# Attention scores on 64-row tiles of TensorE, q and k transposed in one block, and the sink columns of P taken off GpSimd, in a fused attention and two-MoE kernel

## The chip, the core and the metric

The kernel runs as one program on one core of a Trainium2 chip. The metric is the device time of one execution in microseconds (us), the median of several runs. TensorE is called PE here (its weight loads PEld), VectorE DVE, ScalarE ACT, GpSimd POOL, and SyncE, whose queue issues most DMAs, SP.

## What is computed

```python
def reference(...):                         # B=4, H=8, S=768, D=64; sinks 4, window 128
    scores = q @ k.T / sqrt(D)              # per batch and head
    keep   = (key < 4) | (0 <= query - key < 128)
    a = softmax(where(keep, scores, -1e9))
    x = (a @ v)  as 3072 tokens x 512
    x = ((x @ w1) * (x @ w2)) @ w3 @ w_out  # w1, w2: 512x1024; w3: 1024x1024; w_out: 1024x512 (float64 in DRAM)
    logits = x @ w_gate + bias[modality];  e = argmax;  gate = softmax(logits)[e]      # 8 experts
    out = gate * (relu(x @ W1[e]) @ W2[e])  # W1: 512x1024, W2: 1024x512, float32
```

## The kernel before, in words

Products are kept near float32 by splitting each operand into a rounded high part and a rest ("low"), both in the type fp32r, and adding three products: high*high, high*low, low*high. ACT makes the high part, DVE the low one.

The program has four stages, which the profile shows one after the other. **Start** (0 to 129 us): the float64 weights are loaded (`f64_load`), turned into float32 on DVE (`f64_to_f32`), and w3 times w_out is formed on PE (`product`, L289). **First MoE** (129 to 708 us): six groups of 512 tokens; per group 192 matmuls of x with w1 and w2 (L703, tile ab) and 96 with the product of the weights (L691, tile x2p). **Experts** (708 us to the end): seven slots, six of 512 tokens and one of 128; a slot reads which expert and which tokens it has (`decide`, tk and tab), gathers its rows (L859), transposes them (L899), and multiplies by W1 (L912) and W2 (L949), whose parts are loaded as wst by SP (L868, L870). Between them **routing** steps (`route`) compute logits on DVE (L764) and ranks on PE (tile rk).

Attention is cut in 48 units n: 12 stretches of 256 queries by 4 pairs of heads. `att_stream` yields five steps a unit, and the driver `front` weaves them into the start and the first five groups, so that units 0 to 7 fall mostly into the start. A unit before the change: split q and k (`a_split`), transpose the parts with four fp32r transposes each (`a_tq`, `a_tk`), copy q a second time with its halves exchanged (`a_swap`), add the four sink keys to k (kT, on POOL), form scores for two blocks j of 128 queries (`a_scores`: four matmuls each, in which high and low lie on the two halves of the 128 rows), softmax to P, gather P's sink columns as three parts on POOL (psk, L485 and L488) and transpose them (L492), transpose the rest of P (`a_pt`), and multiply by v (`a_pv`: L531, whose two heads write the two halves of the PSUM partitions, and L534 for the sinks).

Within an engine instructions run in the order that the scheduler wrote; a waiting instruction holds all behind it.

Of the kernel before, what the change touches and what calls it, by code (L numbers as in the profile page):

```python
# [26 lines left out]
def attention_moe_moe_kernel(ctx, tc, q, k, v, w1, w2, w3, w_out, mod_id, w_gate, mod_bias, e_w1, e_w2, out,  # L27
# [16 lines left out]
    NS = 4  # L44
    KW = 128 + NS
    banded = n_sink == NS and window == 128

# [46 lines left out]
    neg_r = const.tile([128, 128], F32R, name="neg_r")  # L94
    cur_i = const.tile([128, 128], I32, name="cur_i")
# [12 lines left out]
    ksk = const.tile([128, H, NS], F32R, name="ksk")  # L108
    psk = const.tile([128, 2, 96], F32R, name="psk")
    vst = const.tile([96, NP, 128], F32, name="vst")  # L110

    def consts_early():
# [5 lines left out]
        nc.vector.tensor_scalar(out=neg_r, in0=idf, scalar1=-1.0, scalar2=None, op0=ALU.mult)  # L118
        nc.gpsimd.memset(tmp, 1.0)
# [10 lines left out]
        nc.gpsimd.memset(psk.bitcast(F32), 0.0)  # L130
# [206 lines left out]
    carry = {}  # L337
    xb = mm.tile([128, NP, 2, 3, UNIT], F32R, tag="xb", bufs=1, name="xb")

    def a_load(n):  # L340
        u, p = divmod(n, NP)
        b, c = divmod(u, NC)
        hs = slice(2 * p, 2 * p + 2)
        qn = att.tile([128, 2, 2, D], F32, tag="qn", bufs=2, name="qn")
        kn = att.tile([128, 2, 2, D], F32, tag="kn", bufs=2, name="kn")
        for src, dst in ((q, qn), (k, kn)):
            for j in range(2):
                s0 = c * UNIT + j * 128
                nc.sync.dma_start(out=dst[:, :, j], in_=src[b, hs, s0:s0 + 128, :].rearrange("h s d -> s h d"))
        nat[n] = (qn, kn)  # L350

    def a_load_v(n):
        u, p = divmod(n, NP)
        b, c = divmod(u, NC)
        hs = slice(2 * p, 2 * p + 2)
        vn = att.tile([128, 3, 2, D], F32, tag="vn", bufs=2, name="vn")
# [4 lines left out]
        if c == 0 and p == 0:  # L361
            for kind in range(3):
                for h in range(2):
                    r = kind * 32 + h * NS
                    nc.sync.dma_start(out=vst[r:r + NS, :, h * D:(h + 1) * D],
                                      in_=v[b].rearrange("(p h) s d -> h s p d", h=2)[h, 0:NS])
# [7 lines left out]
    def a_split(n):  # L374
        qn, kn = nat.pop(n)
        qs = att.tile([128, 4, 2, D], F32R, tag="qs", bufs=1, name="qs")
        ks = att.tile([128, 4, 2, D], F32R, tag="ks", bufs=1, name="ks")
        qf = qn.rearrange("p h j d -> p (h j) d")
        kf = kn.rearrange("p h j d -> p (h j) d")
        nc.scalar.activation(out=qs[:, :, 0, :], in_=qf, func=ACTF.Copy, scale=1.0 / float(D) ** 0.5)  # L380
        nc.scalar.activation(out=ks[:, :, 0, :], in_=kf, func=ACTF.Copy)

        def low_parts():
            nc.vector.scalar_tensor_tensor(out=qs[:, :, 1, :], in0=qf, scalar=1.0 / float(D) ** 0.5,
                                           in1=f32(qs[:, :, 0, :]), op0=ALU.mult, op1=ALU.subtract)
            nc.vector.tensor_tensor(out=ks[:, :, 1, :], in0=kf, in1=f32(ks[:, :, 0, :]), op=ALU.subtract)

        stt["low", n] = defer(low_parts)
        stt["s", n] = (qs, ks)

    def a_tq(n):
        qs, ks = stt["s", n]
        stt.pop(("low", n))()
# [3 lines left out]
        qT = att.tile([128, 4, 128], F32R, tag="qT0", bufs=2, name="qT")  # L397
        nc.scalar.activation(out=qT, in_=f32(tp), func=ACTF.Copy)
        stt["q", n, 0] = qT
        stt["tq", n] = tp  # L400

    def a_swap(n):
        qW = att.tile([128, 4, 128], F32R, tag="qT1", bufs=2, name="qW")
        tp = stt.pop(("tq", n))
        for x in range(2):
            nc.scalar.activation(out=qW[x * D:(x + 1) * D], in_=f32(tp[(1 - x) * D:(2 - x) * D]), func=ACTF.Copy)
        stt["q", n, 1] = qW

    def a_tk(n):
        u, p = divmod(n, NP)  # L410
        b, c = divmod(u, NC)
        qs, ks = stt.pop(("s", n))
        tp = ps_t.tile([128, 4, 128], F32R, tag="t", name="tk")
        for i in range(4):
            nc.tensor.transpose(out=tp[:, i, :], in_=ks[:, i].rearrange("p a d -> p (a d)"), identity=idr)
        kT = att.tile([128, 2, 3, KW], F32R, tag="kT", bufs=1, name="kT")
        for h in range(2):
            nc.scalar.activation(out=kT[:, h, 1:3, NS:KW], in_=f32(tp[:, 2 * h:2 * h + 2, :]), func=ACTF.Copy)
        if c == 0:
            nc.gpsimd.tensor_copy(out=ksk[:, 2 * p:2 * p + 2, :], in_=f32(kT[:, :, 1, NS:2 * NS]))  # L420
        s0 = 0 if c else 1
        nc.gpsimd.tensor_copy(out=kT[:, :, s0:3, 0:NS],
                              in_=f32(ksk[:, 2 * p:2 * p + 2, :]).unsqueeze(2).to_broadcast([128, 2, 3 - s0, NS]))
        if c:
            nc.vector.tensor_copy(out=kT[:, :, 0, NS:KW], in_=f32(carry[p]))
        if c < NC - 1:
            cr = att.tile([128, 2, 128], F32R, tag=f"carry{p}", bufs=1, name="carry")
            nc.vector.tensor_copy(out=cr, in_=f32(kT[:, :, 2, NS:KW]))
            carry[p] = cr
        stt["k", n] = kT  # L430

    def a_scores(n, j):
        u, p = divmod(n, NP)
        b, c = divmod(u, NC)
        kT = stt["k", n]
        sp = ps_s.tile([128, 2, 512], F32, tag="s", name="sp")
        blk0 = c == 0 and j == 0
        s0 = 1 if blk0 else j
        for h in range(2):
# [12 lines left out]
        else:  # L452
            nc.vector.copy_predicated(out=sp[:, :, NS:KW], mask=cur_i.unsqueeze(1).to_broadcast([128, 2, 128]),
# [10 lines left out]
        def norm():  # L464
            r = st[:, 2]
            nc.vector.tensor_scalar(out=st[:, 1], in0=st[:, 1], scalar1=1.0e-9, scalar2=None, op0=ALU.add)
            nc.vector.reciprocal(out=r, in_=st[:, 1])
            nc.vector.tensor_tensor(out=P[:, j, :, lo:KW], in0=P[:, j, :, lo:KW],  # L468
# [4 lines left out]
    def a_sk(n):  # L473
# [5 lines left out]
        j0 = 0 if c else 1  # L479
        xp = ps_x.tile([128, 2, 256], F32, tag="x", name="xp")  # L480
        stt["x", n] = xp
        pk = psk.rearrange("p j (a r) -> p j a r", a=3)
        nj = 2 - j0
        for kind in (0, 2):
            nc.gpsimd.tensor_copy(out=pk[:, j0:2, kind, 0:2 * NS].rearrange("p j (h k) -> p j h k", h=2),  # L485
                                  in_=P[:, j0:2, :, 0:NS])
        for j in range(j0, 2):
            nc.gpsimd.tensor_tensor(out=pk[:, j, 1, 0:2 * NS].rearrange("p (h k) -> p h k", h=2),  # L488
                                    in0=P[:, j, :, 0:NS],
                                    in1=f32(pk[:, j, 0, 0:2 * NS]).rearrange("p (h k) -> p h k", h=2),  # L490
                                    op=ALU.subtract)
            nc.tensor.transpose(out=xp[0:96, 1, j * 128:(j + 1) * 128].bitcast(F32R), in_=psk[:, j, :], identity=idr)  # L492
        pt = att.tile([96, 256], F32R, tag="pskT", bufs=1, name="pskT")
        nc.scalar.activation(out=pt[:, j0 * 128:256], in_=xp[0:96, 1, j0 * 128:256], func=ACTF.Copy)
# [23 lines left out]
    def a_pv(n):  # L518
# [5 lines left out]
        sk = stt.pop(("sk", n))  # L524
        spans = [(1, slice(0, 256), parts.rearrange("p a j h q -> p (a j) h q")[:, 0:4:3]),
# [3 lines left out]
        for x, (vj, cols, pm) in enumerate(spans):  # L529
            for h in range(2):  # L530
# [4 lines left out]
                         start=False, stop=True, skip_group_check=True)  # L535
        xh, xl = xb[:, p, 0, u % 3], xb[:, p, 1, u % 3]
        nc.scalar.activation(out=xh, in_=xp[:, 0], func=ACTF.Copy)  # L537
        defer(lambda: nc.vector.tensor_tensor(out=xl, in0=xp[:, 0], in1=f32(xh), op=ALU.subtract))
        stt.pop(("k", n)); stt.pop(("q", n, 0)); stt.pop(("q", n, 1))
# [6 lines left out]
    def att_stream():  # L546
        a_load(0)
        a_load_v(0)
        a_load(1)
        a_vsink(0)  # L550
        a_split(0)
        a_tq(0)
        a_swap(0); yield
        a_tk(0); yield
        for n in range(NN):
            if n + 2 < NN:
                a_load(n + 2)
            if n + 1 < NN:
                a_split(n + 1)
# [4 lines left out]
            if n + 1 < NN:  # L564
                a_tq(n + 1)
                a_swap(n + 1)
# [7 lines left out]
            if n + 1 < NN:  # L574
                a_tk(n + 1); yield
        a_sk(NN - 1); a_pt(NN - 1); yield
        a_pv(NN - 1)
# [415 lines left out]
    def front():  # L993
# [17 lines left out]
        t = 0.0  # L1011
        f64_ahead(4)
# [202 lines left out]
```

## Time and profile before

| what | value |
|---|---|
| median of 3 runs (range) | 1012.94 us (1012.55 to 1014.28) |
| the profiled execution: its time, its span | 1017.59 us, 1015.9 us |
| busy in the span: PE, PEld | 956.0 us (94%), 752.5 us (74%) |
| busy in the span: DVE, ACT, POOL | 644.0 us (63%), 515.8 us (51%), 218.0 us (21%) |
| granted TensorE clock, mean share of full | 0.987 |

The span runs from the first to the last instruction. The end of a matmul is modelled and a matmul overlaps the next, so what a matmul costs PE is read from start to start.

### The profile page before, as it was taken

How to read it: one execution, taken by the hardware profiler on the slowest of the kernel's cores; microseconds unless marked ns; L12 is line 12 of the kernel's file. 1: busy time of each engine (PE TensorE's matmuls, PEld its weight loads, DVE VectorE, ACT ScalarE, POOL GpSimd, SP SyncE). 2: the span in 40 equal slices, each digit the busy share in tenths (PEclk: the TensorE clock that was granted, in tenths of full speed). 3: DMA queues.
4: the chain of work that ended last, by engine and by line, in shares of the span. 5: the costliest groups of instructions: out<-in, count | busy, mean ns of one | idle time of the engine just before them, and what ended most of it. 6: DMA issues, size and time to landing. Idle time of an engine off the chain costs nothing. (4 is left out here: it accounts for less than half of the span.)

```text
span 1015.9 us, 16038 instructions
## 1 busy us (share of the span) xinstructions
PE 956.0 (94%) x4976; PEld 752.5 (74%) x4976; DVE 644.0 (63%) x1968; ACT 515.8 (51%) x1354; POOL 218.0 (21%) x460
## 2 busy tenths in 40 slices
PE   4899799999999999999999999999999997999995
PEld 2667578867786778678867886778888886888884
DVE  7788796489638963895489639847934354343432
ACT  3689665576447644774576445314433414343433
POOL 1232312113223221222122222222031222021010
PEclk9899999999999999999999999999999998999998
DMA  8665624112202220222022200452445306343331
GB/s 262 188 171 167 188 69 131 23 45 63 58 19 49 58 55 19 56 61 52 16 50 59 58 9 16 129 80 63 145 166 117 133 13 236 125 146 117 122 116 52
DMA packets 125417, 94.05 MB, mean 93 GB/s; under 512 B 96712, under 2 KB 105160, under 8 KB 125201
## 3 DMA queue, kind: packets, MB, share of 16 engines
q1 hardware_dynamic: 120560, 80.12, 28.3%
q0 software_dynamic: 4768, 12.88, 4.2%
q8 instruction: 40, 0.66, 0.3%
q14 instruction: 49, 0.39, 0.2%
HBM read 80.14 MB, written 13.09 MB: 92 GB/s over the span
## 5 line engine op out<-in xcount | busy, mean ns | idle before, releaser
L703 PE MATMUL ab<-xb,wab 128*128 128x512 f32 x1152 | 291.0, 397 | 0.4 <-DVE g L713 0.3
L703 PEld LDWEIGHTS ab<-xb,wab 128*128 128x128 f32 x1152 | 210.6, 189 | 41.9 <-ACT xb L537 1.2
L949 PE MATMUL x<-w 128*128 128x512 f32 x600 | 143.1, 396 | 0.0
L764 DVE CUSTOM_DVE_ANT_0 junk<-rows,wgb 128x512 bf16<-128x512 f32 x192 | 134.8, 702 | 1.5 <-ACT rows L751 0.6
L949 PEld LDWEIGHTS x<-w 128*128 128x128 f32 x600 | 113.1, 190 | 23.7 <-DVE w L196 0.3
L691 PE MATMUL x2p<-w3o,gh 128*128 128x512 f32 x384 | 128.2, 407 | 0.0
L461 ACT ACTIVATE P<-sp,st 128x132 f32<-128x132 f32 (+1 forms) x192 | 69.2, 368 | 40.4 <-DVE st L459 26.4
L196 DVE TENSOR_TENSOR w<-wst,w 128x512 fp32r<-128x512 f32 x112 | 71.5, 683 | 25.1 <-ACT w L195 25.1
L513 POOL TENSOR_SCALAR_AFFINE_SELECT ptp<-ptf 128x512 f32<-128x512 f32 (+1 forms) x96 | 63.7, 688 | 107.8 <-ACT ptf L508 107.8
L691 PE MATMUL x2p<-w3o,gl 128*128 128x512 f32 x192 | 76.4, 400 | 0.0
L691 PEld LDWEIGHTS x2p<-w3o,gh 128*128 128x128 f32 x384 | 66.9, 188 | 11.8 <-ACT gh L680 1.9
L912 PE MATMUL ab<-w,w 128*128 128x512 f32 x288 | 75.1, 396 | 0.0
L916 DVE SCALAR_TENSOR_TENSOR w<-ab,w 128x512 fp32r<-128x512 f32 x48 | 33.1, 690 | 65.6 <-ACT w L915 65.4
L195 ACT ACTIVATE w<-wst 128x512 fp32r<-128x512 f32 x112 | 63.5, 628 | 20.9 <-DMA wst<-in_moe_w_dram 20.9
L912 PE MATMUL ab<-w 128*128 128x512 f32 x288 | 74.0, 392 | 0.0
L953 POOL DMA_INDIRECT out_dram<-late,ti x25 | 25.6, 1026 | 217.1 <-ACT late L952 193.0
L680 ACT ACTIVATE gh<-g 128x256 fp32r<-128x256 f32 x96 | 39.9, 415 | 63.0 <-DVE g L710 48.1
L710 DVE TENSOR_TENSOR g<-ab,bs 128x256 f32<-128x256 f32 x48 | 20.2, 421 | 76.6 <-PE ab L703 76.5
L485 POOL CAST psk<-P 128x16 fp32r<-128x16 f32 (+1 forms) x96 | 23.7, 276 | 202.1 <-DVE P L468 149.6
L915 ACT ACTIVATE w<-ab 128x512 fp32r<-128x512 f32 x48 | 28.8, 599 | 74.5 <-PE ab L912 74.1
L912 PEld LDWEIGHTS ab<-w,w 128*128 128x128 f32 x288 | 54.0, 188 | 13.0
L912 PEld LDWEIGHTS ab<-w 128*128 128x128 f32 x288 | 54.0, 188 | 12.1
(195 smaller groups left out, 1685.7 us busy)
## 6 DMA issues: line engine op xcount, KB each, us to landing
wst<-in_moe_w_dram SPq DMA_DIRECT2D x56, 512.0 KB
f64st<-in_moe_w_dram SPq DMA_DIRECT2D x32, 512.0 KB
vn<-in_v_dram SPq DMA_DIRECT2D x128, 64.0 KB
xs<-rows SPq DMA_DIRECT2D x12, 513.0 KB
qn<-in_q_dram SPq DMA_DIRECT2D x96, 64.0 KB
kn<-in_k_dram SPq DMA_DIRECT2D x96, 64.0 KB
f64st<-in_moe_w_out_dram SPq DMA_DIRECT2D x8, 512.0 KB
wgb<-wgt SPq DMA_DIRECT2D x1, 2048.0 KB
```

Of the source, the lines that this page charges most:

```text
L195: nc.scalar.activation(out=hi, in_=src, func=ACTF.Copy)
L196: lo_eng.tensor_tensor(out=lo, in0=src, in1=f32(hi), op=ALU.subtract)
L461: nc.scalar.activation(out=P[:, j, h, lo:KW], in_=sp[:, h, lo:KW], func=ACTF.Exp, bias=st[:, 0, h:h + 1], accum_out=st[:, 1, h:h + 1])
L513: nc.gpsimd.affine_select(out=parts[:, a, i0:2].rearrange("p j h q -> p (j h) q"), in_=full[:, 2 * i0:4], pattern=[[0, 4 - 2 * i0], [sign, ...
L680: nc.scalar.activation(out=gh, in_=g, func=ACTF.Copy)
L691: nc.tensor.matmul(out=x2p[t], lhsT=a[:, sl], rhs=b_, start=(f == 0 and i == 0), stop=(f == KF - 1 and i == 2))
L703: nc.tensor.matmul(out=bank[nm].rearrange("p (u t) -> p u t", u=2), lhsT=a, rhs=b_, start=(kk == 0 and i == 0), stop=(kk == KD - 1 and i = ...
L764: nc.vector.tensor_tensor_reduce(out=junk, in0=rows[:, t, 0:DM], in1=wgb[0][:, e, :], scale=1.0, scalar=0.0, op0=ALU.mult, op1=ALU.add, ac ...
L912: nc.tensor.matmul(out=hp, lhsT=a[:, fs], rhs=b_, start=(kk == 0 and i == 0), stop=(kk == KD - 1 and i == 2))
L915: nc.scalar.activation(out=h[:, 0], in_=hp, func=ACTF.Relu)
L916: nc.vector.scalar_tensor_tensor(out=h[:, 1], in0=hp, scalar=0.0, in1=f32(h[:, 0]), op0=ALU.max, op1=ALU.subtract)
L949: nc.tensor.matmul(out=op, lhsT=a[:, ts], rhs=b_, start=(f == 0 and i == 0), stop=(f == KF - 1 and i == 2))
```

## The change

Five edits, in one diff of some 250 lines.

1. q and k are transposed as loaded, in float32, four transposes into one PSUM bank (`a_tqk`), and split afterwards, out of PSUM. The tiles of k live on in a ring of three blocks per head pair, so nothing is carried over by DVE; the sink keys are copied by POOL once for each batch and pair.
2. The scores take three matmuls per head and block in place of two, each with 64 rows: head 0 on partitions 0 to 63, head 1 on 64 to 127. The first block of a batch has 132 columns instead of 264.
3. P's sink columns are gathered by ACT into a tile skn of 8 columns, transposed in float32 to 8 partitions, and split out of PSUM by two ACT copies and one DVE subtraction (`a_skT`, a step of its own place).
4. For units 0 to 7 (`n < FEW`) the low parts of q, k and x come from PE and ACT (a matmul with a negative identity into the same bank, then a copy), and P is normalised on ACT.
5. The loads of unit 0 go out before the second pair of float64 weights; in the last group routing steps and the decisions of slots 1 to 3 come later, and those of slots 4 to 6 move from slot 2 into slot 3.

```diff
-    def a_tq(n):
-        tp = ps_t.tile([128, 4, 128], F32R, tag="t", name="tq")
-        for i in range(4):
-            nc.tensor.transpose(out=tp[:, i, :], in_=qs[:, i].rearrange("p a d -> p (a d)"), identity=idr)
...
+    def a_tqk(n):
+        tp = ps_t.tile([128, 4, 128], F32, tag="t", name="tqk")
+        for x, src in enumerate((qn, kn)):
+            for j in range(2):
+                i = j if x == 0 or s0 < s1 else 1 - j
+                nc.tensor.matmul(out=tp[:, 2 * x + i], lhsT=src[:, j], rhs=idf, is_transpose=True, start=(x + j == 0),
+                                 stop=(x + j == 2), skip_group_check=True)
...
+            if n < FEW:
+                nc.tensor.matmul(out=tp[:, 0:2], lhsT=negq_r, rhs=qh, start=False, stop=True, skip_group_check=True)
...
-        for h in range(2):
-            for part in range(2):
-                nc.tensor.matmul(out=sp[:, h, 0:2 * KW], lhsT=stt["q", n, part][:, 2 * h + j, :],
-                                 rhs=kT[:, h, s0:s0 + 2, :].rearrange("p a b -> p (a b)"),
-                                 start=(part == 0), stop=(part == 1))
+        for i, (a, b_) in enumerate(((qh, 0), (ql, 0), (qh, 1))):
+            for h in range(2):
+                hp = slice(h * D, (h + 1) * D)
+                nc.tensor.matmul(out=sp[:, h, 0:nk].rearrange("p (a b) -> p a b", b=KW), lhsT=a[hp, j, :],
+                                 rhs=kr[hp, b_, blocks, :], start=(i == 0), stop=(i == 2))
...
-            nc.tensor.transpose(out=xp[0:96, 1, j * 128:(j + 1) * 128].bitcast(F32R), in_=psk[:, j, :], identity=idr)
...
+    def a_skT(n):
...
+            nc.tensor.transpose(out=xp[0:2 * NS, 1, j * 128:(j + 1) * 128], in_=skn[:, j], identity=idf)
...
-            if pos == N_EARLY - 2:
...
+                    if pos == N_EARLY - 1 and f == 2:
```

The order on PE, a unit in the first group of the first MoE (ab and x2p are the MoE's own matmuls; the last figures are output partitions by columns). Before:

```order
L703 MATMUL ab<-xb,wab 128x512 x9
L396 MATMUL tq<-idr,qs 128x128 x4
L691 MATMUL x2p<-w3o,gh 128x512 x2
L691 MATMUL x2p<-w3o,gl 128x512
L441 MATMUL sp<-kT,qT 128x264
L441 MATMUL sp<-kT,qW 128x264
L703 MATMUL ab<-xb,wab 128x512 x12
L531 MATMUL xp<-ptp,vn 64x256 x2
L531 MATMUL xp<-ptp,vn 64x128 x4
L534 MATMUL xp<-pskT,vsk 128x256
L415 MATMUL tk<-idr,ks 128x128 x4
```

And with the change, at the same place:

```order
L715 MATMUL ab<-xb,wab 128x512 x7
L396 MATMUL tqk<-idf,qn 128x128 x2
L396 MATMUL tqk<-idf,kn 128x128 x2
L499 MATMUL xp<-idf,skn 8x128 x2
L703 MATMUL x2p<-w3o,gh 128x512 x2
L443 MATMUL sp<-ring,qh 128x264 x2
L443 MATMUL sp<-ring,ql 128x264 x2
L715 MATMUL ab<-xb,wab 128x512 x12
L543 MATMUL xp<-ptp,vn 64x256 x2
L543 MATMUL xp<-ptp,vn 64x128 x4
L546 MATMUL xp<-pskT_108,vsk 128x256
```

The transposes of k (tk) are gone, the sink transposes stand beside those of q and k, and a block of scores has six matmuls of half the rows (three rows of two) in place of four.

SP's order at the end of slot 2 (wst are expert weights, `TENSOR_LOAD dri` reads a decision and waits for it, tk the token lists). Before:

```order
L870 DMA wst<-in_moe_w_dram 128x2x512
L839 TENSOR_LOAD dri
L840 TENSOR_LOAD dri
L846 DMA tk<-tab_70 128x4
L846 DMA tk<-tab_71 128x4
L1168 TENSOR_LOAD tri
L868 DMA wst<-in_moe_w_dram 128x1024
```

And with the change:

```order
L880 DMA wst<-in_moe_w_dram 128x1024
L882 DMA wst<-in_moe_w_dram 128x2x512
L851 TENSOR_LOAD dri
L852 TENSOR_LOAD dri
L1183 TENSOR_LOAD tri
L858 DMA tk<-tab_70 128x4
L858 DMA tk<-tab_71 128x4
```

The W1 loads of slot 3 (L868 before, L880 now) stood behind the decisions and lists of slots 4 to 6 and now stand ahead of them; rows that repeat are shown once.

## Rows read from the trace of the kernel before

**Rows 1.** Busy time by stage: start (two parts) and first MoE.
```profile
core 0: us, PE busy (x) PEld busy (x) DVE busy (x) ACT busy (x) POOL busy (x), PEclk, DMA share, GB/s
0.00:50.00 50.00, 31.96 (x130) 22.38 (x131) 38.86 (x84) 24.99 (x58) 8.12 (x25) 0.93 0.71 223
50.00:129.00 79.00, 71.18 (x434) 54.08 (x432) 64.31 (x170) 61.38 (x172) 23.57 (x49) 0.98 0.60 172
129.00:633.00 504.00, 492.14 (x2786) 382.17 (x2784) 353.84 (x1204) 294.11 (x874) 116.79 (x294) 1.00 0.20 49
```
**Rows 2.** Groups on PE: busy us, mean ns | idle before, with releasers.
```profile
L441 PE MATMUL sp<-kT,qT 128*128 128x264 f32 x192 | 54.9, 306 | 4.1 <-POOL kT L422 3.6 <-issue 0.3
L531 PE MATMUL xp<-ptp,vn 128*64 128x256 f32 x192 | 36.4, 405 | 3.6 <-POOL ptp L513 3.5
L492 PE MATMUL xp<-idr,psk 128*96 128x128 f32 x80 | 16.1, 249 | 14.7 <-POOL psk L488 14.5
```
**Rows 3.** Timeline of PE in the first MoE: start, length, what, count.
```profile
402.65 0.45 PE L396 MATMUL tq<-idr,qs 128*128 128x128 f32 x4
402.94 0.69 PE L691 MATMUL x2p<-w3o,gh 128*128 128x512 f32 x2
403.47 0.40 PE L691 MATMUL x2p<-w3o,gl 128*128 128x512 f32 x1
...
404.40 0.29 PE L441 MATMUL sp<-kT,qT 128*128 128x264 f32 x1
...
404.89 0.63 PE L691 MATMUL x2p<-w3o,gh 128*128 128x512 f32 x2
...
406.05 0.40 PE L691 MATMUL x2p<-w3o,gl 128*128 128x512 f32 x1
406.37 0.65 PE L531 MATMUL xp<-ptp,vn 128*64 128x256 f32 x2
406.95 0.74 PE L691 MATMUL x2p<-w3o,gh 128*128 128x512 f32 x2
407.53 0.40 PE L691 MATMUL x2p<-w3o,gl 128*128 128x512 f32 x1
```
**Rows 4.** Timeline of PE: a whole product with v, in the start.
```profile
110.65 1.09 PE L531 MATMUL xp<-ptp,vn 128*64 128x256 f32 x12
111.67 0.39 PE L534 MATMUL xp<-pskT,vsk 96*128 96x256 f32 x1
111.89 0.46 PE L415 MATMUL tk<-idr,ks 128*128 128x128 f32 x4
```
**Rows 5.** Timeline of PE: float32 transposes of an expert slot.
```profile
741.84 0.60 PE L899 MATMUL x<-idf,late 128*128 128x128 f32 x4
742.27 0.60 PE L899 MATMUL t<-idf,late 128*128 128x128 f32 x4
```
**Rows 6.** Timeline of PE: the old sink transposes.
```profile
411.78 0.28 PE L492 MATMUL xp<-idr,psk 128*96 128x128 f32 x2
411.89 0.62 PE L504 MATMUL pt<-idf,P 128*128 128x128 f32 x4
```
**Rows 7.** Waits after 640 us: engine line <- releaser: total us, times, longest.
```profile
PE x L899 <- DVE w L196: 5.6, 1, 5.6
PE rk L786 <- DVE oh L775: 2.6, 1, 2.6
```
**Rows 8.** Three stretches with a low granted clock (columns as in rows 1).
```profile
121.50:125.00 3.50, 3.50 (x12) 2.68 (x12) 0.00 (x0) 0.86 (x2) 1.22 (x2) 0.51 0.87 296
660.80:664.20 3.40, 3.06 (x12) 2.48 (x12) 3.05 (x23) 0.60 (x1) 2.77 (x3) 0.51 0.68 30
845.00:851.00 6.00, 4.79 (x16) 4.12 (x17) 5.53 (x9) 4.57 (x9) 2.62 (x3) 0.51 0.91 312
```
**Rows 9.** Timeline of SP's queue at the end of slot 2.
```profile
827.47 8.60 SPq L846 DMA_DIRECT2D tk<-tab  x6
836.94 7.36 SPq L868 DMA_DIRECT2D wst<-in_moe_w_dram  x4
```
**Rows 10.** Groups on DVE in the start, 0 to 129 us.
```profile
L468 DVE TENSOR_TENSOR P<-P,st 128x264 f32<-128x264 f32 x13 | 5.6, 427 | 0.2
L384 DVE SCALAR_TENSOR_TENSOR qs<-qn,qs 128x256 fp32r<-128x256 f32 x10 | 5.1, 514 | 0.0
```

More of the change, by code (lines that the diff above doesn't have):

```diff
@@ L107, in attention_moe_moe_kernel @@
     eidx, ebase, done, tot = (dec[:, x] for x in range(4))
-    ksk = const.tile([128, H, NS], F32R, name="ksk")
-    psk = const.tile([128, 2, 96], F32R, name="psk")
+    pskT = [const.tile([96, 256], F32R, name=f"pskT{x}") for x in range(2)]
     vst = const.tile([96, NP, 128], F32, name="vst")
@@ L129, in consts_early @@
         nc.vector.tensor_copy(out=past_i, in_=tmp)
-        nc.gpsimd.memset(psk.bitcast(F32), 0.0)
+        for x in pskT:
+            nc.gpsimd.memset(x.bitcast(F32), 0.0)
         nc.gpsimd.memset(vst, 0.0)
@@ L360, in a_load_v, with a_load_sinks @@
         stt["v", n] = vn
-        if c == 0 and p == 0:
-            for kind in range(3):
-                for h in range(2):
-                    r = kind * 32 + h * NS
-                    nc.sync.dma_start(out=vst[r:r + NS, :, h * D:(h + 1) * D],
-                                      in_=v[b].rearrange("(p h) s d -> h s p d", h=2)[h, 0:NS])
+        if n and c == 0 and p == 0:
+            a_load_sinks(b)
+    def a_load_sinks(b):
+        for kind in range(3):
+            for h in range(2):
+                r = kind * 32 + h * NS
+                nc.sync.dma_start(out=vst[r:r + NS, :, h * D:(h + 1) * D],
+                                  in_=v[b].rearrange("(p h) s d -> h s p d", h=2)[h, 0:NS])
     def a_vsink(b):
@@ L372, in a_vsink @@
         stt["vsk", b] = vsk
[L374 to L389, printed above, removed]
@@ L409, in a_tk, with low_parts, sinks @@
-    def a_tk(n):
+    def a_tqk(n):
         u, p = divmod(n, NP)
         b, c = divmod(u, NC)
[L412 to L430, printed above, removed]
+        qn, kn = nat.pop(n)
+        if n < NP:
+            ring.append(att.tile([128, 2, 3, KW], F32R, tag=f"ring{p}", bufs=1, name="ring"))
+        kr = ring[p]
+        s0, s1 = 2 * c % 3, (2 * c + 1) % 3
+        blocks = slice(s0, s1 + 1) if s0 < s1 else slice(s1, s0 + 1, s0 - s1)
+        tp = ps_t.tile([128, 4, 128], F32, tag="t", name="tqk")
[4 more added lines that the diff above has]
+                                 stop=(x + j == 2), skip_group_check=True)
+        qh = att.tile([128, 2, 128], F32R, tag="qh", bufs=2, name="qh")
+        ql = att.tile([128, 2, 128], F32R, tag="ql", bufs=2, name="ql")
+        scale = 1.0 / float(D) ** 0.5
+        nc.scalar.activation(out=qh, in_=tp[:, 0:2], func=ACTF.Copy, scale=scale)
+        nc.scalar.activation(out=kr[:, 0, blocks, NS:KW], in_=tp[:, 2:4], func=ACTF.Copy)
+        def low_parts():
+            if n < FEW:
+                nc.tensor.matmul(out=tp[:, 0:2], lhsT=negq_r, rhs=qh, start=False, stop=True, skip_group_check=True)
+                nc.tensor.matmul(out=tp[:, 2:4], lhsT=neg_r, rhs=kr[:, 0, blocks, NS:KW], start=False, stop=True,
+                                 skip_group_check=True)
+                nc.scalar.activation(out=ql, in_=tp[:, 0:2], func=ACTF.Copy, scale=scale)
+                nc.scalar.activation(out=kr[:, 1, blocks, NS:KW], in_=tp[:, 2:4], func=ACTF.Copy)
+                sinks()
+                return
+            nc.vector.scalar_tensor_tensor(out=ql, in0=tp[:, 0:2], scalar=scale, in1=f32(qh), op0=ALU.mult,
+                                           op1=ALU.subtract)
+            nc.vector.tensor_tensor(out=kr[:, 1, blocks, NS:KW], in0=tp[:, 2:4], in1=f32(kr[:, 0, blocks, NS:KW]),
+                                    op=ALU.subtract)
+            sinks()
+        def sinks():
+            if c == 0:
+                nc.gpsimd.tensor_copy(out=kr[:, :, :, 0:NS],
+                                      in_=f32(kr[:, :, 0, NS:2 * NS]).unsqueeze(2).to_broadcast([128, 2, 3, NS]))
+        stt["low", n] = defer(low_parts)
+        stt["q", n] = (qh, ql)
@@ L434, in a_scores @@
         b, c = divmod(u, NC)
-        kT = stt["k", n]
+        if j == 0:
+            stt.pop(("low", n))()
+        kr = ring[p]
+        qh, ql = stt["q", n]
         sp = ps_s.tile([128, 2, 512], F32, tag="s", name="sp")
+        cur = (2 * c + j) % 3
         blk0 = c == 0 and j == 0
-        s0 = 1 if blk0 else j
-        for h in range(2):
-            for part in range(2):
-                nc.tensor.matmul(out=sp[:, h, 0:2 * KW], lhsT=stt["q", n, part][:, 2 * h + j, :],
-                                 rhs=kT[:, h, s0:s0 + 2, :].rearrange("p a b -> p (a b)"),
-                                 start=(part == 0), stop=(part == 1))
+        wrapped = cur == 0 and not blk0
+        blocks = slice(0, 1) if blk0 else slice(0, 3, 2) if wrapped else slice(cur - 1, cur + 1)
+        nk = KW if blk0 else 2 * KW
+        for i, (a, b_) in enumerate(((qh, 0), (ql, 0), (qh, 1))):
+            for h in range(2):
+                hp = slice(h * D, (h + 1) * D)
+                nc.tensor.matmul(out=sp[:, h, 0:nk].rearrange("p (a b) -> p a b", b=KW), lhsT=a[hp, j, :],
+                                 rhs=kr[hp, b_, blocks, :], start=(i == 0), stop=(i == 2))
         if j == 0:
@@ L452, in a_scores @@
         else:
-            nc.vector.copy_predicated(out=sp[:, :, NS:KW], mask=cur_i.unsqueeze(1).to_broadcast([128, 2, 128]),
+            other = past_i if wrapped else cur_i
+            nc.vector.copy_predicated(out=sp[:, :, NS:KW], mask=other.unsqueeze(1).to_broadcast([128, 2, 128]),
                                       data=sp[:, :, KW + NS:2 * KW])
@@ L467, in norm @@
             nc.vector.reciprocal(out=r, in_=st[:, 1])
+            if n < FEW:
+                for h in range(2):
+                    nc.scalar.activation(out=P[:, j, h, lo:KW], in_=P[:, j, h, lo:KW], func=ACTF.Copy,
+                                         scale=r[:, h:h + 1])
+                return
             nc.vector.tensor_tensor(out=P[:, j, :, lo:KW], in0=P[:, j, :, lo:KW],
@@ L479, in a_sk @@
         j0 = 0 if c else 1
+        skn = att.tile([128, 2, 2 * NS], F32, tag="skn", bufs=2, name="skn")
+        nc.scalar.activation(out=skn[:, j0:2].rearrange("p j (h k) -> p j h k", h=2), in_=P[:, j0:2, :, 0:NS],
+                             func=ACTF.Copy)
+        stt["skn", n] = skn
+    def a_skT(n):
+        c = n // NP % NC
+        skn = stt.pop(("skn", n))
         xp = ps_x.tile([128, 2, 256], F32, tag="x", name="xp")
         stt["x", n] = xp
[L482 to L494 removed]
+        cols = slice(0 if c else 128, 256)
+        for j in range(0 if c else 1, 2):
+            nc.tensor.transpose(out=xp[0:2 * NS, 1, j * 128:(j + 1) * 128], in_=skn[:, j], identity=idf)
+        pt = pskT[n % 2]
+        src = xp[0:2 * NS, 1, cols]
+        for kind in (0, 2):
+            nc.scalar.activation(out=pt[kind * 32:kind * 32 + 2 * NS, cols], in_=src, func=ACTF.Copy)
+        stt["sklo", n] = defer(lambda: nc.vector.tensor_tensor(out=pt[32:32 + 2 * NS, cols], in0=src, in1=f32(pt[0:2 * NS, cols]),
+                                                               op=ALU.subtract))
         stt["sk", n] = pt
@@ L1128, in back @@
                     route_step()
-            if pos == N_EARLY - 2:
-                while route_step():
-                    pass
-                for x in range(N_LATE + 1):
-                    slots.append(Slot(SLOT if x < N_LATE else 128, NT, mem))
-                    slots[-1].decide()
-                cnt = trips(p2a_pool[0])
-                n = len(slots)
-                order += list(range(N_EARLY, n))
+                    if pos == N_EARLY - 1 and f == 2:
+                        while route_step():
+                            pass
+                        for x in range(N_LATE + 1):
+                            slots.append(Slot(SLOT if x < N_LATE else 128, NT, mem))
+                            slots[-1].decide()
+                        cnt = trips(p2a_pool[0])
+                        order += list(range(N_EARLY, len(slots)))
             nx = slots[order[pos + 1]] if pos + 1 < len(order) else None
```

67 lines of the change are left out of this document (33 added, 34 removed).

## The prediction

> **What bounds the kernel now.** First read the busy time by stage, to see which engine a stage leans on. In the first MoE PE is busy 492.14 of 504 us, DVE 353.84, ACT 294.11, POOL 116.79 [rows 1]: PE sets that stage, and work taken off the others counts only where PE waits for it. In the start it is mixed: up to 50 us PE is busy 31.96 us against DVE's 38.86, from 50 to 129 us PE 71.18 of 79, DVE 64.31, ACT 61.38 [rows 1].
>
> Then the groups of PE, whose last column is the idle time just before them. POOL's hand in the sink columns costs 14.5 us in front of the sink transposes, 3.6 in front of the scores (sink keys) and 3.5 in front of the product with v [rows 2]. The waits of the last third show two more: 2.6 us for the ranks of a routing step and 5.6 us before the transposes of slot 3 [rows 7]. After these holes the granted clock drops to its lower level, 1.2 GHz: three stretches of 3.4 to 6 us stand at 0.51 [rows 8]. In the first of them PE had just idled for the sink columns, in the second for the ranks, in the third for slot 3.
>
> Last the timeline of PE, since a busy share says nothing of what a matmul costs. Starts, not lengths, are to be compared.
> - Matmuls of 512 columns: from 404.89 to 406.05 there are five (two, and three in rows left out), 1.16 us, 0.23 each [rows 3].
> - Four score matmuls: 404.40 to 404.89, 0.49 us, with nothing lost before or after [rows 3].
> - Four fp32r transposes: 402.65 to 402.94, 0.29, and the next two matmuls take 0.53 instead of twice 0.23: 0.36 together [rows 3].
> - Four float32 transposes: 741.84 to 742.27, 0.43, so 0.11 each [rows 5].
> - Two old sink transposes: 411.78 to 411.89, 0.11 [rows 6].
> - The product with v is the one that shows what tiles of less than 128x128 cost. Two matmuls of 64 output columns stand alone at 406.37. The matmul before started at 406.05 and would have left PE at 406.28; the two after them started at 406.95 and the next at 407.53, 0.58 instead of 0.46, so the stream was whole again as if from 407.07. That is 0.79 us. The two themselves need 0.44 (256 columns at twice the 0.11 us of 128 float32 columns). The rest, 0.35, goes for the change into the narrow tile and back, some 0.18 a change [rows 3, 5].
> - A whole product of 12 such matmuls (4 of 256 and 8 of 128 columns) takes 110.65 to 111.67, 1.02 us, where one after the other would be 1.76 and two heads at a time 0.88 [rows 4]. So two tiles on different halves do run together.
>
> **The change part by part, in PE's time.**
>
> *q and k.* One block of four float32 transposes (0.43) for two blocks of fp32r ones (0.72): -0.29 in 48 units, -14 us.
>
> *Scores, the stream alone.* A block goes from four matmuls (0.49) to six with half the rows. No row of before has tiles of 64 rows. Bounds: the halves run together, three times 0.12 = 0.36; or one after the other, 0.72. I take the first, by the nearest row, the two heads of the product with v [rows 4]. 80 blocks by -0.13 are -10 us; the 16 blocks of 132 columns lie between 0.18 and 0.36, at 0.27 they give -4. Sum -14; one after the other it would be +19.
>
> *Changes of tile.* This is the big term. Counted through the whole order on PE, neighbours with different tiles meet 130 times before (65 products with v, in and out) and 423 times with the change: 201 between full tiles and those of 64 rows, 19 between these and the narrow ones of v, 100 in and out of the sink transposes (8 columns), 103 for v. At 0.18 the 293 more are +53 us. The row shows it for tiles of 64 columns only; for 64 rows the bounds are 0 and 0.18 for each of the 201. I take 0.18. The Trainium skill, page "TensorEngine Tiling (Array Packing)", section "Tiling Modes", says that a change of the tiling mode, not of the tile, drains TensorE; by that all 293 cost, as in my sum, and the trace agrees for the products with v.
>
> *Sink transposes.* 80 of 128 float32 columns at 0.11 are 9 us, for 80 at about 0.06 [rows 6], 5: +4.
>
> *Low parts on PE.* Units 0 to 7 add 24 matmuls of 256 columns. The nearest, L534, takes 0.22 from its start to the next [rows 4], after a change; I take 0.15: +4.
>
> PE's own work thus grows by 53 + 4 + 4 - 14 - 14 = +33 us. Some 63 of the changes fall in the start, where PE stands idle 18 us up to 50 us [rows 1]: 3 us of theirs are hidden there. +30.
>
> **Waits that go.** The sink columns no longer pass POOL: ACT copies 8 columns, and the transposes stand behind those of q and k, in the quoted order after seven ab matmuls, 1.6 us later. All 14.5 goes. The copy of sink keys is left for the first unit of a batch and pair: -3.6. POOL's select for v is no longer queued behind the psk work; half of 3.5, -2 [rows 2]. In the order the awaited rank matmul stands 85 ab matmuls later, some 20 us: -2.6 [rows 7]. SP's W1 loads for slot 3 went out at 836.94, behind six list loads from 827.47 on [rows 9]; they now stand ahead of the decisions, so the 5.6 us before slot 3 go too [rows 7]. What is late next are the lists of slot 4, but that slot begins one slot later. The three low stretches, 12.9 us at half clock, give back half, -6 [rows 8]. Together -34.
>
> **DVE in the start.** The low part of q took 5.1 us there and the normalising of P 5.6 [rows 10]; the low parts of k and x have the shape of q's, so for eight units some 17 us leave DVE. That is worth nothing if PE or ACT take over as the bound (ACT gains the lows and the normalising and loses more copies of q and k, about even), and all 17 if DVE sets the whole start. It is the busiest engine only up to 50 us, and its weight conversions, which stay, are most of that: -6.
>
> **Costed at nothing.** In the first MoE ACT loses six copies of q and k a unit and DVE the carrying of k: both lie beside PE's stream, which does not wait for them [rows 1]. Without that cover they would be a gain. The loads of unit 0 pass SP's queue ahead of the second pair of weights; DVE first converts the first pair, so I set it to 0, with 2 us either way. The later decisions of slots 1 to 3 hold SP, and behind them stand W2 loads of slot 0; in the order two of its four are ahead of them and the third is used halfway through the slot's first stage. If that cover fails, PE waits as it did before slot 3, 5.6 us [rows 7].
>
> **New waits.** The low part is now read from the PSUM bank that P's transposes use next, and the sink part passes ACT, PE, ACT, DVE. All in steps apart; I allow +0 to +8, and take 0, since one bank user a unit (the second transposing block) goes.
>
> Sum: +30 - 34 - 6 = -10 us. The sum is made on an execution of 1017.59 us (1015.9 of them span), 4.7 above the median of 1012.94. The median becomes 1003 us. The own error of these terms is some 10 us.
>
> **The rivals.**
> - *Tiles of 64 rows change for nothing.* For it: the score matmuls of before change weights at every step without loss [rows 3], and no row shows a tile of 64 rows. Against it: the loss at the products with v. Then 201 x 0.18 = 36 us go from the sum: 967 us.
> - *The two halves do not run together* (or their weight loads don't). Each score matmul brings weights of 128 columns of its own; if the second half's load or stream waits for the first's, a pair takes twice 0.12. Then the stream term is +19 and not -14: +33, 1036 us, slower than before. It decides above a third of that, 11 us, that is from 0.16 us for a pair on. Against it: the heads of the product with v do overlap [rows 4].
> - *The float32 sink transposes cost double.* The 64-column matmuls of v take two passes each; if a transpose into 8 columns does as well, 80 x 0.11 = 9 us more, 1012 us, no change. The same page, section "Restrictions and Gotchas", says that column tiling excludes the transpose mode for float32, which would bring this out; no row of before has such a transpose.
>
> **How the numbers follow.** Forecast (993 to 1013 us) 0.50; free changes 0.25; halves apart 0.17; double transposes 0.08. To hold 8 in 10 the range reaches into both outer cases, 964 to 1032 us. What a measurement of this kernel can tell from no change is about 0.2%, 2 us. Faster by more: 0.41 of the forecast's half, the free case and a third of the last, 0.69; within: 0.07; slower: halves apart, and what is left of the others, 0.24.
>
> **What the profile after would show.** Right: in a timeline of the first MoE six score matmuls between two ab blocks cost 0.7 us (0.36 in pairs with equal starts, and 0.18 on either side); the idle before the sink transposes is below 2 us; no hole of 5 us before slot 3's transposes; start shorter by about 5 us; the first MoE's five groups not shorter by more than 10. Wrong: scores at 0.4 us a block (free changes, a first MoE shorter by 30 us), or six even steps of 0.12 (halves apart, first MoE longer by 20). If DVE set the start, the first ab matmul comes well before 120 us.

## The result, and the profile after

The changed kernel takes 990.88 us (median of 4 runs, 990.5 to 991.1) against 1013.24 (4 runs, 1012.55 to 1014.28): ratio 0.978, 95% interval 0.976 to 0.980, so -22.4 us. Forecast were 1003 us, -10. The direction holds and the time lies in the range, but the gain is more than twice the forecast one. The profiled execution took 990.5 us (988.5 of them span).

Busy time by stage, to be read beside [rows 1]; the last two rows are the last group of the first MoE and the experts:

```profile
core 0: us, PE busy (x) PEld busy (x) DVE busy (x) ACT busy (x) POOL busy (x), PEclk, DMA share, GB/s
0.00:50.00 50.00, 34.15 (x155) 23.32 (x155) 40.87 (x89) 26.45 (x70) 6.41 (x22) 0.93 0.79 244
50.00:122.60 72.60, 72.02 (x432) 50.88 (x431) 50.86 (x122) 57.82 (x183) 8.70 (x15) 1.00 0.61 175
122.60:620.40 497.80, 493.66 (x2789) 363.80 (x2788) 355.52 (x1189) 222.62 (x762) 71.88 (x112) 1.00 0.21 49
620.40:690.70 70.30, 69.62 (x327) 55.86 (x326) 50.39 (x206) 21.57 (x46) 19.28 (x22) 1.00 0.30 91
690.70:988.50 297.80, 286.01 (x1304) 234.57 (x1302) 136.38 (x312) 113.66 (x209) 54.69 (x67) 0.99 0.45 129
```

The same three later stages of before:

```profile
129.30:632.50 503.20, 491.34 (x2780) 381.49 (x2779) 353.04 (x1201) 293.39 (x872) 116.79 (x294) 1.00 0.20 49
632.50:708.50 76.00, 71.55 (x332) 57.47 (x331) 51.59 (x206) 21.82 (x46) 19.87 (x34) 0.98 0.42 91
708.50:1015.90 307.40, 289.69 (x1304) 236.74 (x1302) 135.95 (x310) 113.95 (x209) 49.68 (x58) 0.98 0.39 123
```

The start is 6.7 us shorter, the five groups 5.4, the last group 5.7, the experts 9.6: 27.4 between the two profiled executions, of which 4.4 are that the one of before lay above its median (1017.59 against 1013.24 us). In the five groups PE is busy 2.3 us longer and idles 7.7 less (11.9, then 4.1). Over the whole span PE's busy time stays (956.0, then 955.5) and its idle time falls from 59.9 to 33.0. By the forecast's terms idle time was to fall by 37 (28 of waits, 6 in the start, 3 filled by changes of tile there) and PE's own work to grow by 27 (33, less 6 for the clock). Idle time fell by 27; the work did not grow.

Groups on PE, beside [rows 2]:

```profile
L443 PE MATMUL sp<-ring,qh 64*128 64x264 f32 x320 | 53.5, 338 | 3.6 <-ACT P L463 3.5
L543 PE MATMUL xp<-ptp,vn 128*64 128x256 f32 x192 | 37.0, 404 | 0.9 <-POOL ptp L524 0.9
L499 PE MATMUL xp<-idf,skn 128*8 128x128 f32 x80 | 16.9, 273 | 0.3 <-ACT skn L488 0.3
```

The 14.5 us before the sink transposes are 0.3, the 3.6 for the sink keys are gone, the select for v costs 0.9. Of the waits of [rows 7] neither is left: after 640 us PE waits once, 0.5 us. So the waits that the forecast named fell by 28.6 us. New are 3.5 us before the scores, for the exponentials that free their bank, and 1.6 before the transposes of P.

Timeline of PE around a unit, beside [rows 3]:

```profile
402.18 0.71 PE L703 MATMUL x2p<-w3o,gh 128*128 128x512 f32 x2
402.72 0.39 PE L703 MATMUL x2p<-w3o,gl 128*128 128x512 f32 x1
...
403.65 0.38 PE L396 MATMUL tqk<-idf,qn 128*128 128x128 f32 x2
403.87 0.38 PE L396 MATMUL tqk<-idf,kn 128*128 128x128 f32 x2
404.09 0.38 PE L499 MATMUL xp<-idf,skn 128*8 128x128 f32 x2
404.22 0.71 PE L703 MATMUL x2p<-w3o,gh 128*128 128x512 f32 x2
404.87 0.39 PE L443 MATMUL sp<-ring,qh 64*128 64x264 f32 x2
405.09 0.28 PE L443 MATMUL sp<-ring,ql 64*128 64x264 f32 x2
405.21 0.29 PE L443 MATMUL sp<-ring,qh 64*128 64x264 f32 x2
405.43 0.50 PE L703 MATMUL x2p<-w3o,gl 128*128 128x512 f32 x1
405.76 0.63 PE L703 MATMUL x2p<-w3o,gh 128*128 128x512 f32 x2
```

Each x2 of the scores is a pair, one matmul per half. The middle pair takes 0.12 to the next start; the first takes 0.22, the last 0.22, and the full matmul behind them 0.33 in place of 0.23. So the block pays 0.36 for its stream and about 0.2 for each change, as forecast. The surprise is two rows above: the sink transposes start 0.22 after two of k (no loss), the next matmul follows 0.13 later, and the two full matmuls behind them lose no more than behind any float32 transposes, about 0.08 (the two at 402.18 follow transposes of P and take 0.54 in place of 0.46; of the 0.65 from 404.22 on, 0.1 belongs to the scores).

### The profile page after: what moved, and what is told of

It reads as the page before. It is cut to its first block, busy times and chain, and to the rows that moved or that the text cites. A ratio compares the mean times of both kernels' runs of the same rounds, so it can differ in the third digit from the quotient of the medians.

```text
span 988.5 us, 15433 instructions
## 1 busy us (share of the span) xinstructions
PE 955.5 (97%) x5000; PEld 728.4 (74%) x5000; DVE 634.0 (64%) x1913; ACT 442.1 (45%) x1266; POOL 161.0 (16%) x237
## 5 line engine op out<-in xcount | busy, mean ns | idle before, releaser
L961 PE MATMUL x<-w 128*128 128x512 f32 x600 | 141.0, 392 | 0.0
L776 DVE CUSTOM_DVE_ANT_0 junk<-rows,wgb 128x512 bf16<-128x512 f32 x192 | 137.0, 714 | 1.9 <-ACT rows L763 0.5
L443 PE MATMUL sp<-ring,qh 64*128 64x264 f32 (+1 forms) x384 | 62.7, 331 | 3.6 <-ACT P L463 3.5
L443 PEld LDWEIGHTS sp<-ring,qh 64*128 64x128 f32 x384 | 37.5, 185 | 34.6 <-issue 15.1
```

The costliest lines, as they stand in the source:

```text
L443: nc.tensor.matmul(out=sp[:, h, 0:nk].rearrange("p (a b) -> p a b", b=KW), lhsT=a[hp, j, :], rhs=kr[hp, b_, blocks, :], start=(i == 0), st ...
L776: nc.vector.tensor_tensor_reduce(out=junk, in0=rows[:, t, 0:DM], in1=wgb[0][:, e, :], scale=1.0, scalar=0.0, op0=ALU.mult, op1=ALU.add, ac ...
L961: nc.tensor.matmul(out=op, lhsT=a[:, ts], rhs=b_, start=(f == 0 and i == 0), stop=(f == KF - 1 and i == 2))
```

## The experiments

All times are medians beside 990.9 us for the changed kernel and 1013 for the one before. Main theory: the changes of tile at the sink transposes cost nothing, the others do. Rivals: 64-row changes are free; the halves do not overlap; the waits or the start were undersized.

**Full tile for the sink transposes.**
```diff
-        skn = att.tile([128, 2, 2 * NS], F32, tag="skn", bufs=2, name="skn")
+        skn = sknz[n % 2]                  # two zeroed tiles [128, 2, 66], columns 0 to 7 written
-            nc.tensor.transpose(out=xp[0:2 * NS, 1, ...], in_=skn[:, j], identity=idf)
+            nc.tensor.transpose(out=xp[0:66, 1, ...], in_=skn[:, j], identity=idf)
```


> The changed kernel with the sink columns in a zero-padded tile of 66 columns in place of 8, so that their 80 transposes use the full 128x128 tile: the 100 changes of tile into and out of them are gone, and nothing else moves. If each of these changes costs 0.18 us, as the prediction has it, 100 x 0.18 = 18 us go: 973 us against 990.9. If a change into the 8-column tile costs nothing (theory: this is the mis-sized term), the time stays at 991, within 2 us.

992.28 us (991.69 to 992.34). Without its 100 changes of tile the kernel is not 18 us faster but 1.4 slower. That narrow transposes could be cheaper by just what their changes cost is ruled out by PE's timeline of this run, in which the full tile gives the same steps, 0.22 and 0.14:

```profile
404.62 0.38 PE L399 MATMUL tqk<-idf,kn 128*128 128x128 f32 x2
404.84 0.38 PE L502 MATMUL xp<-idf,skn 128*66 128x128 f32 x2
404.98 0.71 PE L706 MATMUL x2p<-w3o,gh 128*128 128x512 f32 x2
```

The 100 changes cost nothing.

**Changes between full and 64-row tiles.** Behind the first and the second pair of a block (second run: both behind the last pair):
```diff
+            if i < 2:
+                nc.tensor.matmul(out=sp[:, i, 384:512], lhsT=neg_r, rhs=idr, start=False, stop=False, skip_group_check=True)
```


> The changed kernel with two more small matmuls (full tile, 128 columns of fp32r, unused columns of the score bank) per block of scores, one after the first pair and one after the second: 192 matmuls and 384 changes between full and 64-row tiles more. Work of the added matmuls alone 192 x 0.06 = 12 us. If a change between full and 64-row tiles costs 0.18 us: 69 us on top, 1072 us. If it is free (rival): 1003 us.

> The same two added matmuls per block, both behind the last pair, where a full tile follows anyway: no change of tile more (or nearly none). Both theories: 991 + 12 = 1003 us. The difference of the run with the matmuls between the pairs and this one is 384 changes: 69 us by 0.18 each, 0 if they are free.

1068.22 us between the pairs, 1019.3 behind them: 48.9 us for 368 changes (784 against 416 in the two orders), 0.13 each. They are not free, so that rival falls. The price of the added matmuls was misjudged: 28 us for 192, not 12. Some 5 of the 28 are more idle time of PE (38.0 against 33.0 us); by PE's busy time (978.1 against 955.5 us) a small matmul costs 0.12 and not 0.06. Timeline of PE in the first run, where each L446 stands between two changes:

```profile
420.76 0.39 PE L443 MATMUL sp<-ring,qh 64*128 64x264 f32 x2
421.08 0.33 PE L446 MATMUL sp<-idr,neg_r 128*128 128x128 f32 x1
421.33 0.39 PE L443 MATMUL sp<-ring,ql 64*128 64x264 f32 x2
```

A pair and a small matmul repeat every 0.57 us. With 0.12 for the pair's stream and 0.12 for the small matmul, 0.33 are left for two changes, 0.17 each (an estimate).

**Heads apart, and the pairs twice.**
```diff
-        for i, (a, b_) in enumerate(((qh, 0), (ql, 0), (qh, 1))):
-            for h in range(2):
+        for h in range(2):
+            for i, (a, b_) in enumerate(((qh, 0), (ql, 0), (qh, 1))):
```


> The changed kernel with the six score matmuls of a block in the order of heads (three of head 0, then three of head 1) in place of pairs: only the third and the fourth lie on different halves and stand next to each other. If halves run together, a block takes 5 x 0.12 in place of 3 x 0.12: 80 blocks by 0.24 and 16 by 0.12, +21 us, 1012 us. If they do not run together anyway (rival): 991 us.

993.83 us, only 3 us more: my expectation failed. By itself this would fit halves that never overlap, but PE's timeline of this run shows the opposite, pairs all the same:

```profile
306.01 0.39 PE L443 MATMUL sp<-ring,qh 64*128 64x264 f32 x2
306.24 0.29 PE L443 MATMUL sp<-ring,ql 64*128 64x264 f32 x2
306.36 0.28 PE L443 MATMUL sp<-ring,qh 64*128 64x264 f32 x2
306.57 0.50 PE L703 MATMUL x2p<-w3o,gl 128*128 128x512 f32 x1
```

The first matmul of head 1, issued behind three of head 0, starts with the first of head 0. In some blocks of this run other matmuls stand between the heads, and one half runs alone:

```profile
613.86 0.39 PE L443 MATMUL sp<-ring,qh 64*128 64x264 f32 x1
614.09 0.28 PE L443 MATMUL sp<-ring,ql 64*128 64x264 f32 x1
614.21 0.28 PE L443 MATMUL sp<-ring,qh 64*128 64x264 f32 x1
```

Its steps, 0.23 and 0.12, are those of the pairs. That the overlap is real and not only how starts are recorded was tested by more work:
```diff
-        for i, (a, b_) in enumerate(((qh, 0), (ql, 0), (qh, 1))):
+        for i, (a, b_) in enumerate(((qh, 0), (ql, 0), (qh, 1)) * 2):
```


> The changed kernel with the three pairs of score matmuls of every block issued twice (the second time overwrites the first, same result): 576 matmuls more, no change of tile more. If the halves run together, 80 blocks by 0.36 us and 16 by 0.18 to 0.36: 32 to 35 us more, about 1024 us. If they run one after the other: twice that, about 1058 us.

1038.77 us, +47.9, between the two expectations. PE's timeline of this run decides:

```profile
324.25 0.39 PE L443 MATMUL sp<-ring,qh 64*128 64x264 f32 x2
324.48 0.28 PE L443 MATMUL sp<-ring,ql 64*128 64x264 f32 x2
324.60 0.41 PE L443 MATMUL sp<-ring,qh 64*128 64x264 f32 x4
324.85 0.28 PE L443 MATMUL sp<-ring,ql 64*128 64x264 f32 x2
324.97 0.28 PE L443 MATMUL sp<-ring,qh 64*128 64x264 f32 x2
325.18 0.66 PE L515 MATMUL pt<-idf,P 128*128 128x128 f32 x4
```

From 324.25 to 325.18 six pairs take 0.93, three took 0.56 above: 0.37 for three, 0.12 a pair. That is some 35 of the 47.9 us; the rest is idle time of PE (46.1 us against 33.0, in the five groups 14.6 against 4.1), which came with the longer blocks. The halves run together.

**Width or transposing?** The sink tile zero-padded to 64 columns, the tile of v; then the plain product with the identity in place of the transposing mode, in 8 and in 66 columns:
```diff
-            nc.tensor.transpose(out=xp[0:2 * NS, 1, ...], in_=skn[:, j], identity=idf)
+            nc.tensor.matmul(out=xp[0:2 * NS, 1, ...], lhsT=skn[:, j], rhs=idf, start=True, stop=True)
```


> The changed kernel with the sink columns zero-padded to 64 columns in place of 8, so that the transposes use the same tile as the product with v (97 and 106 changes between it and the full tile in place of 47 and 56). If width matters (a change into a 64-column tile costs 0.18 us, one into 8 columns nothing): 100 x 0.18 = +18 us, 1009 us. If it is the transposing that makes the change free: 991 to 993 us.

> The changed kernel with the 80 sink transposes as plain products with the identity (8 columns as before; float32, two passes, 0.22 in place of 0.11 us: +9 us by that alone). If the transposing made the 96 changes free, a product pays 0.18 for each: +9 +17, 1017 us. If a change into a tile of 8 columns is free for any matmul: 1000 us.

> The same plain products in 66 columns, in the full tile, without the 96 changes: 991 + 9 = 1000 us by both theories. What the run in 8 columns takes more than this one is the changes alone: 17 us if a product pays 0.18 for each, 0 if the width of 8 columns makes them free.

992.13 us for transposes of 64 columns: free as well. The products take 1008.61 in 8 columns and 1000.99 in 66: 7.6 us for 96 changes, 0.08 each over the whole kernel; so it is the transposing, not the width. PE's timeline with the product in 8 columns (two passes each, so x4):

```profile
423.27 0.38 PE L396 MATMUL tqk<-idf,kn 128*128 128x128 f32 x2
423.58 0.60 PE L499 MATMUL xp<-idf,skn 128*8 128x128 f32 x4
424.11 0.73 PE L703 MATMUL x2p<-w3o,gh 128*128 128x512 f32 x2
```

And with that in 66 columns:

```profile
417.95 0.38 PE L399 MATMUL tqk<-idf,kn 128*128 128x128 f32 x2
418.17 0.60 PE L502 MATMUL xp<-idf,skn 128*66 128x128 f32 x4
418.52 0.71 PE L706 MATMUL x2p<-w3o,gh 128*128 128x512 f32 x2
```

0.31 and 0.53 against 0.22 and 0.35: 0.27 us for two changes, where the transposes lose none.

**The kernel before, once more.**

> The kernel before, unchanged, for a second profiled execution: the first took 1017.59 us, 4.7 above the median, and the sum of the prediction was made on it. Theory: part of the waits that the sum lets go (5.6 us before slot 3, 2.6 for the ranks, the three low-clock stretches) are not in every execution; a profiled execution near the median, 1013 us, shows them shorter by about 4.7 us together. Rival: the 4.7 us are spread evenly over the stages, and the holes stand as they did.

1013.69 us; its profiled span is 1013.2. Its waits after 640 us, beside [rows 7]:

```profile
PE x L899 <- DVE w L196: 4.9, 1, 4.9
PE rk L786 <- DVE oh L775: 1.7, 1, 1.7
```

1.6 us less, of the 2.7 by which this profiled execution is shorter than the first.

**The end alone**, in the kernel before: `next_early` from 47000 on, `due = min(t, 46000) / 1100`, and the decisions of slots 4 to 6 in slot 3.

> The kernel before with the last part of the fifth edit alone (routing steps and decisions of slots 1 to 3 later in the last group, decisions of slots 4 to 6 in slot 3). By the prediction's terms it takes 2.6 (ranks), 5.6 (slot 3) and about 4 (two of the three low-clock stretches, half of 9.4 us): -12 us, 1001 us against 1013. If the holes of the profiled execution are larger than in the median (theory): -7 to -9, 1004 to 1006 us. If the decisions only wait elsewhere: 1013 us.

1003.83 us, ratio 0.992 (0.990 to 0.994): -9.2 us. Both holes are gone (after 640 us PE waits once, 0.5 us), the last group takes 72.7 us and the experts 298.8. The edit works at some 9 us, not 13.

**The start's work on DVE again:** `FEW = 0`.

> The changed kernel without its fourth edit: in units 0 to 7 the low parts of q, k and x come from DVE and P is normalised there, 24 matmuls on PE fewer. By the prediction the edit is worth -6 us (DVE) and +4 (PE, partly hidden in the start): 993 to 997 us. If DVE sets the whole start (rival, 17 us): above 1000. If PE sets it: 987 to 991 us.

991.24 us: no difference. The first ab matmul stands at 121.1 us, even before the changed kernel's 122.6; from 50 us on DVE is then busy 59.6 of 71 us, PE 69.8. PE sets this stretch, DVE does not.

**The loads of unit 0 late again:** `f64_ahead(4)` ahead of `a_load(0)`, `a_load_v(0)`.

> The changed kernel with the loads of unit 0 behind the second pair of float64 weights again (first part of the fifth edit undone). By the prediction: 0, with 2 us either way, 989 to 993 us. If the earlier loads are what made the start shorter (rival): 994 to 997 us, the first matmul of the first MoE up to 6 us later.

993.28 us (990.96 to 993.83), the first ab matmul 3.4 us later: 2.4 us, at the edge of what can be told.

**The old place of the sink transposes:** `a_skT(n)` called at the end of `a_sk`.

> The changed kernel with the sink transposes where they stood before: right behind the copy of the sink columns and ahead of the transposes of P, and not a step later. The copy is still ACT's. If the place took the wait away (theory: PE must come to the transposes late enough), PE waits again for the normalising of P and ACT's copy, some 0.3 us in 48 units or more: +10 to +15 us, 1001 to 1006 us. If it was POOL's four steps (rival): within 2 us of 991.

996.19 us, +5.3, between the two. PE's waits in the first MoE then (columns as in [rows 7]):

```profile
PE pt L516 <- DVE P L475: 3.0, 5, 0.7
PE xp L500 <- ACT skn L488: 0.7, 2, 0.3
```

In the first MoE of before, the sink transposes waited 7.6 us; here they wait 0.7, at the old place. So taking POOL's steps out did away with nearly all of that wait. The place is worth 5.3 us beside it, in waits of the neighbours: before the transposes of P 3.0 us against 1.2, before the product with v 2.5 (POOL's select) against 0.9.

**The product with v behind the scores:** `a_pv(n - 1)` directly after `a_scores(n, 1)`, both yields behind it.

> The changed kernel with the product with v right behind the second block of scores (a step earlier), so that in 19 units the scores are followed by it without a full tile between: 396 changes of tile in place of 423, none of the 27 in the sink transposes save 3. At 0.2 us for each of the 24: -5 us, 986 us, if the earlier product meets no wait for its parts (POOL's select for v). With such waits: 991 to 996 us.

988.42 us (987.95 to 988.59): 2.5 us faster than the change, half of what was expected, and the fastest version of this study. Waits of 1.9 us before the product (reason "issue") are new.

**Scores in full tiles.** `a_tqk` writes per head qT (high over low), qW (low over high) and the ring of k in 64-partition copies; `a_scores` becomes:
```diff
+        for h in range(2):
+            for i, a in enumerate(stt["q", n]):
+                nc.tensor.matmul(out=sp[:, h, 0:nk].rearrange("p (a b) -> p a b", b=KW), lhsT=a[:, h, j, :],
+                                 rhs=kr[:, h, blocks, :], start=(i == 0), stop=(i == 1))
```


> The changed kernel with the scores in full tiles again, as before (high and low part of a head on the two halves of the 128 rows, two matmuls per head), but out of the new float32 transposes: ACT, DVE and POOL write the parts of q twice and of k once into stacked tiles, some 8 copies of 64 partitions a unit in place of 4 of 128. The 201 changes into and out of 64-row tiles are gone. If the changes are what a block of scores pays (0.76 against 0.50 us, row for row): 96 by 0.26 is -25 us, and the copies lie beside PE's stream in the first MoE: 966 us, or up to 980 if the start, where ACT and DVE are nearer to PE, pays for them. If the changes cost little: 990 us or more.

1009.58 us (1003.96 to 1013.54), a clear miss. The first group is shorter, 89.9 us against 97.3, but later PE waits for POOL's copies, 9.2 us in three holes for qW and 2.8 in one for the ring, and behind three of the four it runs at the lower clock. PE's timeline around the longest of these holes:

```profile
580.05 0.28 PE L437 MATMUL sp<-ring,qT 128*128 128x264 f32 x1
584.24 0.59 PE L437 MATMUL sp<-ring,qW 128*128 128x264 f32 x1 [3.91 <-POOL qW L412]
...
585.08 1.05 PE L697 MATMUL x2p<-w3o,gh 128*128 128x512 f32 x2
585.93 0.63 PE L697 MATMUL x2p<-w3o,gl 128*128 128x512 f32 x1
```

The two x2p matmuls take 0.43 each in place of 0.23. POOL's timeline of the same stretch tells why the copy is late:

```profile
573.77 0.97 POOL L804 DMA_INDIRECT tab<-tokid,ix  x1 [0.30 <-issue]
583.79 0.85 POOL L412 CAST qW<-qT 64x256 fp32r<-64x256 f32 x2 [9.05 <-DMA tab<-tokid,ix]
```

By the profile POOL stood idle for 9.05 us until its scatter of token numbers (`tab`, a routing step) had landed, and the copy stood behind that. Ahead of the other three holes it waited 7.6 to 8.4 us for the same. So the miss comes at least in part from one queue, not from the number of copies; the copies on another engine were not tried. This run also has two buffers for v in place of three and one for qW (space); what that costs by itself was not tried.

## Why the prediction was half as large as the result

**The step that failed** is "Changes of tile", in the count: "100 in and out of the sink transposes (8 columns)" at 0.18, 18 of the 53 us. The price was read from products (v) and laid on transposes. Measured: 0 (992.3 without these changes, 990.9 with them), and 0 at 64 columns, while products into the same 8 columns pay. The rule of the Trainium skill that the forecast set beside its sum (page "TensorEngine Tiling (Array Packing)", section "Tiling Modes": a change of the tiling mode drains TensorE) agrees with the runs for products, 0.08 to 0.2 us a change. If transposes into 8 columns change the mode, it does not hold for them, and the measurement decides. The Trainium skill, same page, section "Restrictions and Gotchas", has column tiling and the float32 transpose mode exclude each other. That would fit transposes that are simply never tiled; it is argued, not shown.

**Right, with its size:** the scores. Block 0.77 us against 0.72 forecast (404.22 to 405.76, less three full matmuls of 0.23 and 0.08 behind the transposes), pairs with equal starts, 0.2 a change. The rivals "64 rows change for free" and "halves apart" both fall. q and k: 0.44 for four, 0.43 forecast. The five groups are not shorter by more than 10 us (5.4).

**Third rival:** the float32 transposes into 8 columns do not cost double. Two take 0.13 us to the next start and 0.08 lost behind it, 0.21 together or about 0.11 each, as forecast; double would be 0.44.

**Waits that go:** the sink columns, sink keys and the select went as forecast. **New waits**, taken at 0 within 0 to 8 us, came to 5 (3.5 before the scores, 1.6 before the transposes of P). The end was over-sized: 2.6, 5.6 and half of the two later low stretches, 4.7, are 12.9; the run with that edit alone gives 9.2. About 1.6 of the difference is that the waits are shorter in an execution nearer the median.

**DVE in the start, -6,** was wrong as a reason. The start is 6.7 us shorter, but with DVE's work put back it stays short. What had held PE there is the wait for the sink columns: before, one of 4.9 us stood at its end, with the first low stretch behind it [rows 8]. The row of before:

```profile
121.39 0.50 PE L492 MATMUL xp<-idr,psk 128*96 128x128 f32 x2 [4.91 <-POOL psk L488]
```

The 4.9 us and half of that stretch's 3.5 are 6.7, as much as the start became shorter; now PE is busy 72.02 of 72.6 us. I counted that wait in the 14.5 and then a gain of DVE beside it. The edit with its low parts on PE, forecast -6 and +4, is worth 0.

Summed anew: -10, less 18 for the changes that are free, plus 4 for the end, plus 2 for the start: -22 us; measured -22.4. That the sum closes this well is luck. It leaves out the 5 us of new waits, and the price of the 193 changes that are left over those of before is known only as 0.13 to 0.2 us: at 0.13 in place of 0.18 they cost 10 us less (an estimate). PE's own work should by the forecast still have grown by 9 us without the 18, and it did not grow; a lower price would fit that, but no run shows it.

## What to carry to other kernels

Ask of a price not only which tile it was read from but which operation: here a change of tile cost 0.1 to 0.2 us around products and nothing around float32 transposes into 8 or 64 columns, and a count times a price turned that into the largest error of the sum. Where a hole in front of the bounding engine lies in a stage, count the stage's gain once, as the hole; the load of the other engines there is worth something only after it. And relief that rests on more copies must be weighed with the queue in which the last of them stands, not with busy shares: POOL was 20% busy in the run with full-tile scores, and its copies came up to 4 us late because its queue waited for a DMA.

## What the runs showed of the hardware

- Matmuls on the two 64-row halves of PE start together even when three of one half are issued ahead of those of the other: starts in pairs 0.12 us apart in both orders, 993.8 against 990.9 us. One half alone has the same steps, 0.23 and 0.12.
- Float32 transposes into a tile of 8 or 64 columns paid no change of tile (990.9 and 992.1 us, against 992.3 in the full tile); plain products into 8 columns paid 7.6 us for 96 changes.
- Small products (128 columns of fp32r) between larger ones cost 0.12 us each of PE's busy time (22.6 us for 192), twice the 0.06 of the old sink transposes [rows 6].
- Behind the hole of 3.9 us in the run with full-tile scores, the granted clock of the next 3.2 us was 0.52, its lower level of 1.2 GHz, and 512 columns took 0.43 us in place of 0.23.
